# A mask built as bytes among the first constants, two PSUM banks held from one unit earlier, and new orders on all engines

## The chip, the cores and the metric

The kernel runs on one core of one Trainium2 chip. The metric is the device time of one execution in microseconds. The kernel is one straight program: nothing loops at run time on the path that is taken, and each engine (TensorE = PE, VectorE = DVE, ScalarE = ACT, GpSimd = POOL, and SyncE = SP, which issues all DMAs) works through its own list of instructions in a fixed order and waits on semaphores for the others.

## The reference, cut to what matters

```python
def _attn_ref(q, k, v, a_re, a_im):            # (B=4, H=8, S=768, D=48)
    mag = sqrt(a_re**2 + a_im**2); scale = minimum(mag, 0.999) / (mag + 1e-6)
    ar, ai = a_re * scale, a_im * scale
    for t in range(S):                          # complex state S_re, S_im of D x D for each head
        new_re = ar[t, :, None] * S_re - ai[t, :, None] * S_im
        new_im = ar[t, :, None] * S_im + ai[t, :, None] * S_re
        S_re, S_im = new_re + outer(k[t], v[t]), new_im
        y[t] = q[t] @ S_re
def _moe_ref(x, w_in, w_out):                   # x: 3072 x 384, w_in: 384 x 2048, w_out: 2048 x 384
    h = x @ w_in
    return (h * tanh(softplus(h))) @ w_out
```

The first part is a linear recurrence with a complex decay for each row of the state; its output, with the heads side by side, is the x of the second part. The weights come as 8-byte whole numbers that hold doubles, and are turned into floats on the chip.

## The kernel before

The 768 time steps of a batch are cut into 3 units of 256 steps, so there are 12 units, each of two chunks of 128 steps. A unit goes through three stages, and all engines work on several units at once:

- **The decay** (`ew_steps`): the magnitude and the angle of the decay are summed along time (DVE scans), and q and k are multiplied by growth and by cosine and sine. ACT needs two of its function tables for it: one with logarithm and exponential (`l`), one with sine and arctangent (`t`). Line 240 asks for each load of a table by name (`SETS`, `l` and `t` in turn, 43 loads). Within a unit the angle's arctangent needs `t`, the magnitude's Ln and Exp need `l`, the sines need `t` again. For unit 0 the two chunks (g = 0, 1) go apart. The products with sine and cosine (line 466, tiles X and QK) are laid out anew by SP's DMAs as tile T (line 462, three DMAs of X and three of QK for each chunk), which has 96 rows for each head.
- **The attention of a chunk** (`attn_steps`): PE turns k (`pkn`, line 553; ACT copies it to `kn`, line 554), multiplies k by q (`pa`, line 597; from unit 3 on in 32-row pieces, line 592), DVE masks the result into `am` (line 599 with the causal mask `cmask`; from unit 3 on by a predicated copy through `turned_mask`, line 593, into an `am` that was zeroed before), PE makes the output (`ypsum`, line 612; ACT copies it to `y`, line 617) and the state's update (`pd`, line 632; DVE makes S of it, lines 637 to 640). SP sends y on as `xf` (lines 653, 666).
- **The two dense layers** (`moe_steps`): 8 pairs of columns a unit; PE `ph` (lines 695, 699), a chain on ACT and DVE (lines 703 to 709, tiles e, g, gh, gl), PE `po` (lines 732, 736). In units 0 and 1 half of the work uses the weights `raw` as whole floats; the others use two parts (`w`) that DVE and ACT cut them into (`divide`). Before that, each of the 16 blocks of weights is made a float by ACT (line 278), DVE (lines 280, 281) and POOL (line 283).

PE also runs 84 matmuls on nothing (`junk`, line 516: 40 that wait for the first angle, 44 more), which keep it busy. What stands in a row on an engine is set by hand: the table `ORDER` holds one list of numbers for each engine, and `in_order` ties each instruction to the one before it in the list.

PSUM banks: `bank` (line 530) gives the attention its banks under the tag `pa`, of which there are two. Up to unit 2 each use takes a new tile of the pool; from unit 3 on (`PU` = 3) two tiles are held for good and used in turn, and DVE sets each to zero when it is taken (line 535). The mask for the predicated copy is made when unit 3 first needs it: POOL sets an `am` (floats) to one, cuts it with eight selects, casts it to bytes, and sets the two `am` to zero (lines 577 to 585).

Of the kernel before, what the change touches and what calls it, by code (L numbers as in the profile page):

```python
# [120 lines left out]
    """,  # L121
    "DVE": """
# [70 lines left out]
    """,  # L193
}

SETS = "l t l t l t l t l t l t l t l t l t l t l t l t l t l t l t l t l t l t l t l t l t l"

# [798 lines left out]
```

## Time and profile before

| | us |
|---|---|
| median of 3 runs | 573.54 (572.95 to 574.87) |
| the profiled execution | 572.68 |
| its span in the trace | 570.9 |

| engine | busy, us | share of the span |
|---|---|---|
| PE | 545.7 | 96% |
| DVE | 475.6 | 83% |
| ACT | 467.4 | 82% |
| POOL | 46.5 | 8% |

The trace counts times from the start of the span. A row of the timeline merges a run of like instructions and tells in brackets how long the engine stood idle ahead of it and what ended that. A row of a window tells how long each engine was busy in one stretch. Since PE works in a fixed list, its end is the start of its first true matmul, plus its work, plus the time that it then waits.

### The profile page before, as it was taken

The numbers are of one execution on the slowest core, as the hardware profiler recorded it, in microseconds if no ns is written. First come the engines' busy times: TensorE is split into PE (matmuls) and PEld (weight loads), VectorE is DVE, ScalarE is ACT, GpSimd is POOL, SyncE is SP. The second block draws the span as 40 slices with busy tenths as digits, with TensorE's granted clock in tenths as the row PEclk, the third lists the DMA queues.
The fourth block names the chain that finished last, engine by engine and source line by source line (L and its number), as shares of the span: only waits on it lengthen the run. The fifth ranks groups of instructions, "written<-read, shape, count | busy, mean of one in ns | idle before, by whom it ended". The sixth has DMA issues, their size and how long they took to land.

```text
span 570.9 us, 14394 instructions
## 1 busy us (share of the span) xinstructions
PE 545.7 (96%) x5830; PEld 506.1 (89%) x5830; DVE 475.6 (83%) x795; ACT 467.4 (82%) x749; POOL 46.5 (8%) x60
## 2 busy tenths in 40 slices
PE   0799999999999999999999999999999999999996
PEld 0367877889999999999999999999999999999996
DVE  5999999999999898887989899777897788545543
ACT  7899898999979899978898997787988867646571
POOL 2022322234002000000000000000000000000000
PEclk9999999999999999999999999999999999999999
DMA  8666865815655645606635727517334535301000
GB/s 296 225 195 220 311 195 151 239 56 148 188 172 153 189 155 142 187 28 170 190 108 141 200 74 214 149 38 220 93 109 125 160 99 147 112 30 29 3 26 32
DMA packets 69063, 81.65 MB, mean 143 GB/s; under 512 B 6144, under 2 KB 60672, under 8 KB 68992
## 3 DMA queue, kind: packets, MB, share of 16 engines
q1 hardware_dynamic: 68992, 80.68, 48.2%
q8 instruction: 47, 0.77, 0.6%
q14 instruction: 24, 0.20, 0.1%
HBM read 45.51 MB, written 11.40 MB: 100 GB/s over the span
## 4 chain that ended last, share of the span: by engine, by line
PE 64%; DVE 13%; ACT 12%; DMA 5%; issue 3%; SPq 2%; DVEq 0%; ACTq 0%
PE po L736 27%; PE ph L699 27%; PE ypsum L612 5%; PE pp L592 3%; ACT L240 3%; DMA raw<-w_out 2%; PE pp L632 2%; DVE g L709 2%; DVE X L419 1%; DVE w L249 1%; DMA raw<-w_in 1%; ACT R L482 1%; DVE gl L249 1%; SPq L462 1%; DMA T<-X 1%
## 5 line engine op out<-in xcount | busy, mean ns | idle before, releaser
L699 PE MATMUL ph<-xH,w 128*128 128x256 f32 x1104 | 216.4, 286 | 0.5 <-DVE g L709 0.4
L736 PE MATMUL po<-w,gh 128*128 128x384 f32 x704 | 193.6, 339 | 0.0
L699 PEld LDWEIGHTS ph<-xH,w 128*128 128x128 f32 x1104 | 177.6, 191 | 3.8 <-issue 1.2
L699 PE MATMUL ph<-xL,w 128*128 128x256 f32 x552 | 156.9, 284 | 0.3 <-DVE xL L249 0.3
L736 PEld LDWEIGHTS po<-w,gh 128*128 128x128 f32 x704 | 127.6, 188 | 1.3 <-issue 0.6
L736 PE MATMUL po<-w,gl 128*128 128x384 f32 x352 | 118.2, 337 | 0.0
L699 PEld LDWEIGHTS ph<-xL,w 128*128 128x128 f32 x552 | 105.2, 191 | 2.0 <-DVE xL L249 0.9
L703 ACT ACTIVATE e<-ph 128x512 f32<-128x512 f32 (+1 forms) x100 | 57.2, 573 | 37.2 <-PE ph L699 32.6
L705 ACT ACTIVATE e<-e 128x512 f32<-128x512 f32 (+1 forms) x100 | 60.8, 611 | 30.8 <-DVE e L704 30.7
L709 DVE SCALAR_TENSOR_TENSOR g<-e,ph 128x512 f32<-128x512 f32 (+1 forms) x100 | 65.7, 660 | 19.6 <-ACT e L707 18.3
L736 PEld LDWEIGHTS po<-w,gl 128*128 128x128 f32 x352 | 66.1, 188 | 0.3 <-DVE gl L249 0.2
L249 DVE TENSOR_TENSOR gl<-g,gh 128x512 fp32r<-128x512 f32 x88 | 59.9, 684 | 5.6 <-ACT gh L248 5.3
L707 ACT ACTIVATE e<-e 128x512 f32<-128x512 f32 (+1 forms) x100 | 60.9, 612 | 2.1
L706 ACT ACTIVATE e<-e 128x512 f32<-128x512 f32 (+1 forms) x100 | 60.9, 611 | 1.8
L704 DVE TENSOR_SCALAR e<-e 128x512 f32<-128x512 f32 (+1 forms) x100 | 41.1, 413 | 24.2 <-ACT e L703 23.7
L240 ACT ACT_TABLE_LOAD x43 | 55.2, 1283 | 1.6 <-PEq L950 0.8
L516 PE MATMUL junk<-cmask 128*128 128x512 bf16 x84 | 23.1, 419 | 14.3 <-DVE I L425 14.3
L283 POOL TENSOR_TENSOR raw<-raw 128x768 int32<-128x768 int32 x16 | 26.7, 1675 | 87.2 <-DVE raw L281 29.1
L612 PE MATMUL ypsum<-T,S 96*48 96x128 f32 x320 | 32.3, 277 | 0.0
L516 PEld LDWEIGHTS <-cmask 128*128 128x128 bf16 x84 | 8.7, 106 | 24.1 <-issue 17.9
L593 DVE COPY_PREDICATED am<-tmask,pp 128x512 f32<-128x512 uint8 x36 | 25.8, 734 | 4.3 <-PE pp L592 4.3
L248 DVE CAST gh<-g 128x512 fp32r<-128x512 f32 x48 | 20.6, 429 | 10.2 <-PE po L736 10.0
(103 smaller groups left out, 848.6 us busy)
## 6 DMA issues: line engine op xcount, KB each, us to landing
T<-X SPq DMA_DIRECT2D x72, 129.0 KB, 2.6
T<-QK SPq DMA_DIRECT2D x72, 129.0 KB, 2.5
raw<-w_in SPq DMA_DIRECT2D x8, 768.0 KB, 6.4
raw<-w_out SPq DMA_DIRECT2D x8, 768.0 KB, 7.4
kd<-vx SPq DMA_DIRECT2D x45, 128.0 KB, 2.2
kn<-kd SPq DMA_DIRECT2D x15, 384.0 KB, 3.3
V<-v SPq DMA_DIRECT2D x12, 384.0 KB, 5.2
out_dram<-o SPq DMA_DIRECT2D x24, 192.0 KB, 2.5
```

The source lines that it names most:

```text
L240: nc.scalar.preload_act_table_set({"l": "natural_log_exp_and_others", "t": "trig_and_small"}[name])
L249: leng(out=lo, in0=src, in1=h.bitcast(F32), op=ALU.subtract)
L516: ins = nc.tensor.matmul(junk, cmask, cmask.unsqueeze(1).broadcast_to([P, 4, P]), start=True, stop=True)
L612: nc.tensor.matmul(py[64 * par:64 * par + D, i, :], lhs, rhs, start=n == 0, stop=first or n == 1)
L699: nc.tensor.matmul(ph[:, a, :], rows_in(parts[j][:, wp], kt, a), st[xp][:, kt, :], start=n == 0, stop=n == 8)
L703: act(e, ph, AF.Exp)
L704: nc.vector.tensor_scalar_min(e, e, math.exp(20.0))
L705: act(e, e, AF.Square, bias=1.0)
L706: act(e, e, AF.Ln, scale=0.2, bias=0.2)
L707: act(e, e, AF.Exp, scale=-1.0)
L709: nc.vector.scalar_tensor_tensor(g, e, 2.5, ph, ALU.subtract, ALU.mult)
L736: nc.tensor.matmul(po[t], gp[:, a, tsl], rows_out(parts[NPAIR + j][:, wp], a), start=j in starts and a == 0 and n == 0, stop=j + 1 in ends ...
```

## The change

1. `turned_mask` is made among POOL's first constants, as bytes (int8, read as uint8 by the copy): one memset and eight selects on bytes. The memset to one, the eight selects on floats and the cast in unit 3 are gone; the two memsets of `am` to zero stay.
2. `bank` holds its two tiles from unit 2 on (`u >= PU - 1`), which writes them whole first; DVE's two memsets of line 535 are gone.
3. `SETS` has two more table loads, 45 for 43.
4. `ORDER` has new lists. PE's list is another up to entry 2102 (some 200 us into the span) and the same from there on; it holds the same instructions, 84 `junk` among them. The lists of DVE, ACT, POOL and SP are another over about the same stretch.

```diff
 ORDER = {
     "PE": """
-        0+20 48+4 40+4 52+4 20+2 56+4 44+4 60+15 22+13 124+4 75+5 128+2 35 132+4 130 188+6 36+2 226+3 38 80+5 136+4 85
+        0+20 40+2 48+6 44 54+2 20+3 56+8 45+3 42+2 23+12 64+12 124+6 35 76+4 132+4 36 188+6 130 226 131 248 80+10
...
-SETS = "l t l t l t l t l t l t l t l t l t l t l t l t l t l t l t l t l t l t l t l t l t l"
+SETS = "l t l t l t l t l t l t l t l t l t l t l t l t l t l t l t l t l t l t l t l t l t l t l"
...
-    turned_mask = const.tile([P, 4, C], U8, name="tmask")
+    turned_mask = const.tile([P, 4, C], mybir.dt.int8, name="tmask")
+    nc.gpsimd.memset(turned_mask, 1.0)
+    for i, lo, hi in ((0, 0, 128), (1, 0, 32), (1, 32, 64), (1, 64, 128), (2, 0, 64), (2, 64, 128), (3, 0, 96), (3, 96, 128)):
+        nc.gpsimd.affine_select(out=turned_mask[lo:hi, i], in_=turned_mask[lo:hi, i], compare_op=ALU.is_ge, fill=0.0,
+                                base=-((lo - 32 * i) % P), pattern=[[1, C]], channel_multiplier=-1)
...
         def bank(shape, use, name, c):
-            if u >= PU:
+            if u >= PU - 1:
                 if len(banks) < 2:
                     banks.append(ps.tile([P, 4 * C], F32, tag="pa", name="pp", bufs=2))
-                    nc.vector.memset(banks[-1], 0.0)
...
                             am = at.tile([P, 4, C], F32, tag="am", name="am", bufs=2)
-                            if not masked:
-                                nc.gpsimd.memset(am, 1.0)
-                                for i, lo, hi in (...):
-                                    nc.gpsimd.affine_select(out=am[lo:hi, i], ...)
-                                nc.gpsimd.tensor_copy(turned_mask, am)
                             nc.gpsimd.memset(am, 0.0)
...
-                        nc.vector.copy_predicated(am, turned_mask, pa)
+                        nc.vector.copy_predicated(am, turned_mask.bitcast(U8), pa)
```

What stands in a row at three places. The first is ACT in the opening, from the end of the first logarithms of unit 0 (X_145 or X_156 and X_146 or X_157 are unit 0's two work tiles, R and I its decay, raw the weights). Before:

```order
L370 ACTIVATE X_145<-X_145 128x384
L278 ACTIVATE raw_152<-raw_152 128x768
L406 ACTIVATE X_146<-R_139 128x3x128
L407 ACTIVATE X_146<-R_139 128x3x128
L240 ACT_TABLE_LOAD
L482 ACTIVATE I_140<-I_140 128x384
L368 ACTIVATE X,good<-R 128x3x128
L371 ACTIVATE X_146<-I_140 128x3x128
L368 ACTIVATE X,good<-R 128x3x128
L482 ACTIVATE R_139<-I_140 128x384
L482 ACTIVATE X_145<-I_140 128x384
L482 ACTIVATE R_139<-R_139 128x384
```

And of the change, from the same place (the lines are four later):

```order
L244 ACT_TABLE_LOAD
L486 ACTIVATE I_151<-I_151 128x384
L375 ACTIVATE X_157<-I_151 128x3x128
L282 ACTIVATE raw_163<-raw_163 128x768
L244 ACT_TABLE_LOAD
L410 ACTIVATE X_157<-R_150 128x3x128
L374 ACTIVATE X_156<-X_156 128x384
L411 ACTIVATE X_157<-R_150 128x3x128
L244 ACT_TABLE_LOAD
L486 ACTIVATE X_156<-I_151 128x384
L486 ACTIVATE I_151<-I_151 128x384
L486 ACTIVATE R_150<-I_151 128x384
```

The first arctangent (L482, now L486, of I) goes ahead of the magnitude's last exponentials, and that takes two more table loads; the second chunk's arctangent now stands with the first chunk's sines, behind the third of these loads. Behind the piece of the change come one more Square (L372), the last sine and a load.

The second place is SP in the opening, from the first DMA of T on. Before:

```order
L462 DMA T<-X_146 16x8x258
L324 DMA QK<-k 128x3x128
L324 DMA QK<-q 128x3x128
L462 DMA T<-X_146 16x8x258 x2
L462 DMA T<-QK 16x8x258 x3
```

And of the change, where the other load of q now stands among the first loads:

```order
L466 DMA T<-X_157 16x8x258 x3
L466 DMA T<-QK 16x8x258
L328 DMA QK<-k 128x3x128
L466 DMA T<-QK 16x8x258 x2
L321 DMA R<-a_re 128x768
```

One load, not two, now stands between the six DMAs that PE's first true work needs. The same place ahead of it has a load of q in third position, in front of the second load of R and the first weights.

The third place is POOL. Before, in unit 3:

```order
L578 MEMSET am 128x512
L283 TENSOR_TENSOR raw_1063<-raw_1063 128x768
L581 AFFINE_SELECT am<-am 64x128
L581 AFFINE_SELECT am<-am 32x128
L581 AFFINE_SELECT am<-am 96x128
L581 AFFINE_SELECT am<-am 32x128
L581 AFFINE_SELECT am<-am 128x128
L585 MEMSET am 128x512
L581 AFFINE_SELECT am<-am 32x128
L581 AFFINE_SELECT am<-am 64x128 x2
L584 CAST tmask<-am 128x512
L585 MEMSET am 128x512
```

And of the change, in the opening, from the last of the old constants (`ident`) to the first weights:

```order
masks.py:199 AFFINE_SELECT ident<-ident 96x96
L235 MEMSET tmask 128x512
L237 AFFINE_SELECT tmask<-tmask 128x128
L237 AFFINE_SELECT tmask<-tmask 64x128
L237 AFFINE_SELECT tmask<-tmask 32x128 x3
L237 AFFINE_SELECT tmask<-tmask 64x128
L287 TENSOR_TENSOR raw_163<-raw_163 128x768
```

The memset and six of the eight selects stand in the opening, ahead of POOL's first work on weights; the other two stand between later blocks of weights.

## Rows read from the trace of the kernel before

**Rows 1.** Windows: length; busy (count) of PE, PEld, DVE, ACT, POOL; clock, DMA, GB/s.
```profile
3.88:31.88 28.00, 13.60 (x76) 7.38 (x76) 25.12 (x54) 24.82 (x48) 1.46 (x1) 0.94 0.79 266
24.40:31.90 7.50, 6.73 (x56) 4.94 (x56) 7.44 (x17) 5.98 (x14) 0.00 (x0) 0.77 0.84 300
31.90:53.30 21.40, 20.39 (x187) 14.85 (x187) 21.26 (x41) 20.60 (x35) 5.30 (x4) 1.00 0.64 196
53.30:205.00 151.70, 150.67 (x1464) 133.78 (x1465) 148.35 (x242) 135.29 (x219) 32.87 (x30) 1.00 0.61 182
205.00:566.00 361.00, 361.00 (x4106) 350.12 (x4104) 279.69 (x458) 285.43 (x448) 5.01 (x14) 1.00 0.41 114
```

**Rows 2.** Timeline of PE: start, duration, line, operation, count, idle before, releaser.
```profile
24.43 1.13 PE L597 MATMUL pa<-T 96*128 96x128 f32 x8 [3.24 <-DMA T<-QK]
30.56 0.64 PE L612 MATMUL ypsum<-am,V 128*48 128x128 f32 x8 [0.70 <-DVE am L599]
37.66 0.54 PE L695 MATMUL ph<-xf,raw 128*128 128x128 f32 x3
53.31 0.60 PE L553 MATMUL pkn<-ident,T 96*128 96x96 f32 x5 [0.89 <-DMA T<-X]
117.30 0.36 PE L699 MATMUL ph<-xH,w 128*128 128x256 f32 x1 [0.36 <-DVE g L709]
189.56 0.39 PE L699 MATMUL ph<-xL,w 128*128 128x256 f32 x1 [0.33 <-DVE xL L249]
```

**Rows 3.** Timeline of ACT in the opening.
```profile
7.10 0.51 ACT L369 ACTIVATE X<-X 128x384 f32<-128x384 f32 x1
8.62 0.91 ACT L278 ACTIVATE raw<-raw 128x768 int32<-128x768 uint32 x1 [0.46 <-DMA raw<-w_in]
9.43 0.51 ACT L406 ACTIVATE X<-R 128x384 f32<-128x384 f32 x1
9.84 0.51 ACT L407 ACTIVATE X<-R 128x384 f32<-128x384 f32 x1
10.37 1.28 ACT L240 ACT_TABLE_LOAD   x1
11.66 0.52 ACT L482 ACTIVATE I<-I 128x384 f32<-128x384 f32 x1
31.88 0.59 ACT L617 COPY y<-ypsum 112x512 f32<-112x512 f32 x1
32.36 0.85 ACT L368 ACTIVATE X<-R 128x768 f32<-128x768 f32 x1
```

**Rows 4.** Timeline of DVE: the product QK of unit 0, and of unit 1.
```profile
17.23 0.96 DVE L466 TENSOR_TENSOR QK<-QK,R 128x768 f32<-128x768 f32 x1
47.16 0.95 DVE L466 TENSOR_TENSOR QK<-QK,R 128x768 f32<-128x768 f32 x1
```

**Rows 5.** Timeline of SP's queue: first and last DMA of unit 0's T.
```profile
16.86 0.71 SPq L462 DMA_DIRECT2D T<-X  x1
20.14 1.84 SPq L462 DMA_DIRECT2D T<-QK  x3
```

**Rows 6.** By line: DVE memsets and masked copies: ns min/median/max, first, last start.
```profile
L535 DVE MEMSET pp<- x2: 485/485/485, 128.3 to 138.6; 128x512 f32 x2
L593 DVE COPY_PREDICATED am<-tmask,pp x36: 708/734/754, 152.3 to 502.9; 128x512 f32<-128x512 uint8 x36
```

**Rows 7.** POOL: a constant's select, weights, unit 3's mask; DVE beside the weights.
```profile
1.76 0.29 POOL L230 TENSOR_SCALAR_AFFINE_SELECT cmask<-cmask 128x128 bf16<-128x128 bf16 x1
10.67 1.46 POOL L283 TENSOR_TENSOR raw<-raw 128x768 int32<-128x768 int32 x1 [8.13 <-DVE raw L281]
35.52 3.21 POOL L283 TENSOR_TENSOR raw<-raw 128x768 int32<-128x768 int32 x2 [23.39 <-ACT raw L278]
128.42 2.57 POOL L581 TENSOR_SCALAR_AFFINE_SELECT am<-am 64x128 f32<-64x128 f32 x5
35.59 1.82 DVE L280 TENSOR_SCALAR wx<-raw 128x768 uint32<-128x768 uint32 x1
```

More of the change, by code (lines that the diff above doesn't have):

```diff
@@ L75 @@
     "PE": """
[45 rows of a table removed]
[45 rows of a table added]
     """,
     "DVE": """
[27 rows of a table removed]
[27 rows of a table added]
     """,
     "Activation": """
[22 rows of a table removed]
[22 rows of a table added]
     """,
     "Pool": """
-        5 3+2 1 7 0 6 2 8 10 9 11 56 12+2 15 14 17 16 18+6 27 26 25 28 24 33 36 35 30 29 39 31 34 32 37+2 40+8 49 48
-        51 50 52+2 55 54
+        14 3+2 1 16 0 15 2 5+2 11 7 13 8+2 17 19 18 20+3 24 23 12 26+2 25 10 28+2 31 30 32 34 33 36 35 37+2 55 40 39
+        41+6 48 47 50 49 51+2 54 53
     """,
     "SP": """
[13 rows of a table removed]
[13 rows of a table added]
     """,
 }
-SETS = "l t l t l t l t l t l t l t l t l t l t l t l t l t l t l t l t l t l t l t l t l t l"
+SETS = "l t l t l t l t l t l t l t l t l t l t l t l t l t l t l t l t l t l t l t l t l t l t l"
 def in_order(tc, nc):
@@ L576, in f @@
                             am = at.tile([P, 4, C], F32, tag="am", name="am", bufs=2)
-                            if not masked:
-                                nc.gpsimd.memset(am, 1.0)
-                                for i, lo, hi in ((0, 0, 128), (1, 0, 32), (1, 32, 64), (1, 64, 128),
-                                                  (2, 0, 64), (2, 64, 128), (3, 0, 96), (3, 96, 128)):
-                                    nc.gpsimd.affine_select(
-                                        out=am[lo:hi, i], in_=am[lo:hi, i], compare_op=ALU.is_ge, fill=0.0,
-                                        base=-((lo - 32 * i) % P), pattern=[[1, C]], channel_multiplier=-1)
-                                nc.gpsimd.tensor_copy(turned_mask, am)
                             nc.gpsimd.memset(am, 0.0)
```

212 rows, old and new, of the table ORDER are left out of this document.

## The prediction, written before the change was run

> **What bounds the kernel now.** I read the windows first, for where PE waits, then PE's own timeline for what it waits for, then the opening on ACT, DVE and SP. PE's first true matmul starts at 24.43, behind 3.24 us of idleness that a DMA of T ends [rows 2]. From there on PE is idle for 7.50 - 6.73 = 0.77 us up to 31.9, 1.01 up to 53.3, 1.04 up to 205 and not at all after that [rows 1]: 2.8 us in all. The last 361 us are work alone. The change keeps PE's instructions, the 84 empty ones among them, so the end can move by three things only: the start at 24.43, these 2.8 us, and new waits of PE ahead of 205 us. DVE is the other full engine: 21.26 of 21.40 us busy, then 148.35 of 151.70 [rows 1], so what comes late from ACT or SP makes DVE late, and it has little room to catch up. ACT has some room: 24.82 busy of 28.00 us in the opening, so 3.2 us idle [rows 1].
>
> **The first rows of T.** Instructions of ACT on 384 columns start 0.41 us apart (9.43, 9.84), and a table load takes 1.28 us, with the next instruction 0.01 us behind it (10.37 to 11.66) [rows 3]. The new list switches at the end of the logarithm, 7.10 + 0.51 = 7.6. Load to 8.9; arctangent; Square; the copy of the weights' low part at 9.7 for 0.91 (its DMA had landed at 8.62, and now has one load of 192 KB more ahead of it: at the window's 266 GB/s 0.7 us, so 9.3, still in time); load from 10.6 to 11.9; three Exp, of which DVE holds none up, to 13.25; load to 14.5; sine, arctangent of the second chunk, Abs, Square, last sine, which ends near 16.9. DVE's product with it then ends near 17.9; before it ended at 17.23 + 0.96 = 18.19 [rows 4]. The other product (X) ends near 17.05. SP issued eight DMAs from 16.86 to 21.98, 0.64 us each [rows 5]; now the same stretch holds seven, from 17.07: 17.07 + 7 x 0.64 = 21.55. PE started 2.45 us behind the last issue, which gives 24.0. Term: **-0.43 us** on PE's first true work. Two loads more on ACT there cost 2.57 us, and what hides them is idle time and the second chunk's arctangent, which no longer needs a switch of its own.
>
> **From there to the first dense layer.** PE's first `ph` at 37.66 is a fixed point: it needs y, copied by ACT at 31.88, and DMAs behind that, 5.78 us in all [rows 2, 3]. Ahead of that copy ACT now does 2.57 us of loads and the Square that stood behind it (0.85 us and its accumulator), and leaves two copies of kn, 384 columns each, for later (0.41 us each): net 2.8 us. If all 3.2 us of idle time take it up, the copy starts at 31.5; if none does, at 34.7. Carried on by the same steps along ACT and DVE, I get 32.2, near the lower end, since the two longest waits of ACT in that stretch were for angles which now come earlier. So `ph` starts near 38.0: +0.3 us. The copies of kn come some 3 us later, so on PE the state's update waits; the new list has 12 empty matmuls ahead of it, and its result is needed only by the next chunk.
>
> **Unit 1, and DVE from there on.** The same steps put unit 1's first arctangent at 38.0 and its QK product at 46.7 to 47.65 where it was 47.16 to 48.11 [rows 4]; the last DMA of its T goes out 0.35 us earlier, and PE's wait at 53.31 [rows 2] ends at 52.95. There PE would be 0.35 us ahead. DVE is not: with its scan of the first magnitude behind the weights' DMA (about 1 us idle near 8.5) and two waits for exponentials, I find it 0.65 us behind at 53 us, for equal work. From 60 to 117 us its list holds the same work ahead of each product that PE takes (to within 0.3 us for `g`), so it stays behind by as much, and at 117.30, where PE already waited 0.36 us for `g` [rows 2], PE takes DVE's lateness over: **+0.65** at most, -0.35 at least. These are sums over some sixty instructions, good to about 1 us.
>
> **The memsets of the two banks** took 0.485 us each, at 128.3 and 138.6 [rows 6]: up to 0.97 us of DVE, less some overlap. That is more than the 0.65 us, and DVE is level from there. PE has no wait between 117 and 189, so it gains nothing directly; at 189.56 it waits 0.33 us for `xL` [rows 2], which hangs on a DMA of xf, and a PE that comes 0.65 later finds that wait gone. So of +0.65 about +0.3 is left.
>
> **The mask.** POOL's work at 128 us (five selects 2.57 us [rows 7], three more, a memset, a cast) goes; nothing waits for it, since the mask is first used at 152.3 [rows 6]. In the opening the memset and six selects are priced by the select of 0.29 us [rows 7]: about 2.3 us, done by 5, and POOL idles 8.13 us there, up to its first weights at 10.67 [rows 7]. What can cost there is DVE. One row shows a DVE instruction on 768 columns taking 1.82 us beside POOL's work on weights (35.59 beside 35.52 [rows 7]); one on as many columns with two inputs took 0.96 [rows 4], so at least 0.86 us was lost. With byte selects of 0.3 us such a meeting costs 0 to 0.3 us, and DVE waits for ACT in that stretch; I take 0.
>
> The Trainium skill has a rule for this (SBUF — State Buffer, section "Who interferes with whom"): a DVE instruction with two inputs in SBUF and a GpSimd instruction that reads SBUF shut each other out for a whole instruction. It speaks against moving the selects beside unit 0's first DVE instructions, which read R twice. By it the sum would get up to 0.3 us, as above.
>
> **The held banks.** Unit 2 uses two tiles in turn as it did two buffers, and a bank is still free when its last reader is done. If tracking inside one tile releases a region earlier or later, the bound is the 0.73 us of a masked copy [rows 6] either way; I take 0.
>
> **The sum.** From -0.35 to +0.65 at PE, with +0.3 after 189 us and nothing that moves the rest: between 572.3 and 573.3 against the profiled 572.68. Take +0.15; the profiled execution lies 0.86 below the median, so 573.7 for the median. That is no change: 0.3% is 1.7 us, about what a measurement can tell from none.
>
> **Rivals.** *Slower: the loads are not absorbed.* If ACT's idle time in the opening is not where the loads fall, y is copied up to 2.8 us late, `ph` starts late by as much, and PE has no slack afterwards to win it back: 573.5 + 2.8 = 576.3. It decides from a copy later than 33.6. For it: as I carry it on, ACT's new list has hardly a pause between 17 and 32. Against it: the second arctangent needs no wait now, and the wait of 0.46 us at 8.62 [rows 3] is filled. 0.22.
>
> *Slower by more: a switch costs more than its load.* If each switch cost as much again as its load, the two would take 5.1 us, 2 us over ACT's idle time at the very least, and y would come 2.2 to 5.4 us late: 575.7 to 578.9. Against it: the next instruction stands 0.01 us behind the load, with nothing idle ahead of it (9.84 + 0.51 = 10.35, load at 10.37) [rows 3]. 0.03. The Trainium skill (ScalarE: Activation LUTs, section "What ACT_TABLE_LOAD costs") is such a rule: 1283 ns for the load, and about 1380 ns for a drain with it. The row agrees with the load's time and shows no drain.
>
> *Faster: the new order takes PE's waits away.* All that PE can win is 0.43 + 2.8 = 3.2 us, 570.3; if the waits at 30.56, 53.31, 117.30 and 189.56 (0.70, 0.89, 0.36, 0.33 [rows 2]) go, that is 0.43 + 2.28 = 2.7, 570.8. For it: my sum has an error of about 1 us, the second mask (`am` of 30.56) comes earlier in it, and the clock, 0.77 in that window [rows 1], costs PE there something that closer work would give back. Against: more than half of all PE's waits must go, and `ph` hangs on y. 0.25.
>
> *The change does not do what it says.* The memsets and the selects are gone from the lists, so this is left only for the use of it: DVE's 0.97 us may be worth nothing since PE sets the end. My forecast has that in it.
>
> **How the numbers follow.** Forecast of no change 0.50, at 573.7, own range 572.0 to 575.2; faster by over 0.3% 0.25; slower by over 0.3% 0.25. The range 570.8 to 576.3 goes from the faster case's time to that of the slower one, and leaves out what is beyond either.
>
> **What would show it.** Right: T's first matmul near 24.0; four table loads before 14.5; y copied between 31.5 and 33; `ph` near 38; from 205 us on PE without a gap; `am` of unit 3 untouched by POOL at 128. Wrong: y copied after 33.6; a new wait of PE over 1 us between 24 and 140; PE's clock at its lower level (1.2 GHz) for longer than in the window from 24.4 to 31.9, since the new order leaves PE idle more between 26 and 29 us; DVE at 117 us later by more than 1.5 us, or earlier.

## The result, and the profile after

The changed kernel takes 576.03 us (median of 8 executions, 575.22 to 578.87); the kernel before takes 572.91 in the same comparison (8 executions, 571.89 to 574.87). The ratio is 1.0056, with a 95% interval of 1.0037 to 1.0076: **slower, by some 3.1 us**. That lies inside the range of the prediction, 0.3 us from its upper end, but it isn't the likeliest case. The profiled execution took 575.68 us with a span of 574.0 us, against 572.68 and 570.9.

The windows of the changed kernel, over the same stretches as [rows 1] (length; busy time and count of PE, PEld, DVE, ACT, POOL; clock, DMA, GB/s):

```profile
3.88:31.88 28.00, 12.82 (x62) 6.56 (x63) 24.35 (x54) 26.66 (x49) 3.02 (x6) 0.94 0.75 258
24.40:31.90 7.50, 5.79 (x42) 4.03 (x43) 7.50 (x20) 7.44 (x15) 0.00 (x0) 0.77 0.82 288
31.90:53.30 21.40, 19.95 (x194) 13.94 (x192) 21.20 (x40) 21.12 (x37) 5.33 (x3) 1.00 0.65 192
53.30:205.00 151.70, 149.50 (x1456) 131.73 (x1453) 146.78 (x238) 132.86 (x214) 26.61 (x23) 1.00 0.60 180
205.00:566.00 361.00, 360.32 (x4111) 350.20 (x4110) 280.82 (x461) 288.00 (x453) 4.21 (x14) 1.00 0.42 117
```

PE is idle for 1.71, 1.45, 2.20 and 0.68 us in the last four stretches; before it was 0.77, 1.01, 1.03 and 0 [rows 1]. That is 3.2 us more (0.94, 0.44, 1.17 and 0.68), which is the whole loss. The clock is the same as before in each stretch, so in this pair of executions it is no part of the difference. What PE waits for (engine, line, releaser: us, times, the longest):

```profile
PE junk L520 <- DVE I L429: 15.5, 1, 15.5
PE pkn L556 <- DMA T<-QK: 3.2, 1, 3.2
PE pkn L556 <- DMA T<-X: 2.0, 1, 2.0
PE ph L690 <- DMA xf<-y: 0.9, 1, 0.9
PE ypsum L607 <- DVE am L594: 0.7, 2, 0.4
PE ph L694 <- DVE g L704: 0.6, 2, 0.4
PE po L731 <- DVE gl L253: 0.2, 1, 0.2
```

Three rows of PE's timeline in the changed kernel:

```profile
25.75 0.35 PE L556 MATMUL pkn<-ident,T 96*128 96x96 f32 x2 [3.16 <-DMA T<-QK]
...
39.40 0.87 PE L690 MATMUL ph<-xf,raw 128*128 128x128 f32 x5 [0.91 <-DMA xf<-y]
...
55.77 0.27 PE L556 MATMUL pkn<-ident,T 96*128 96x96 f32 x1 [2.00 <-DMA T<-X]
```

The first true matmul comes at 25.75 and not at 24.43 [rows 2]: 1.32 us late; in the rest of that stretch PE then waits less than before. The wait for unit 1's T grew from 0.89 us [rows 2] to 2.00, and the first `ph` comes 1.7 us later, behind a DMA of xf. From 205 us on PE is idle for 0.68 us, mostly in waits for DVE, where before it never was.

The opening shows why it is late. DVE's timeline in the changed kernel:

```profile
6.49 0.56 DVE L370 SCALAR_TENSOR_TENSOR X<-R 128x384 f32<-128x384 f32 x1 [0.35 <-DMA R<-a_re]
9.68 0.56 DVE L284 TENSOR_SCALAR wx<-raw 128x768 uint32<-128x768 uint32 x1 [1.15 <-DMA raw<-w_in]
13.74 1.19 DVE L380 TENSOR_TENSOR I<-I,X 128x384 f32<-128x384 f32 x1 [0.67 <-ACT X L374]
18.51 0.96 DVE L470 TENSOR_TENSOR QK<-QK,R 128x768 f32<-128x768 f32 x1
```

ACT's, in the same stretch:

```profile
10.15 0.53 ACT L375 ACTIVATE X<-I 128x384 f32<-128x384 f32 x1 [0.58 <-DMA I<-a_im]
10.58 0.88 ACT L282 ACTIVATE raw<-raw 128x768 int32<-128x768 uint32 x1
```

And POOL's, the selects of the mask and the first weights, with one of the selects by itself (count, ns min/median/max, start):

```profile
3.08 2.61 POOL L237 TENSOR_SCALAR_AFFINE_SELECT tmask<-tmask 128x128 int8<-128x128 int8 x6
...
L237 POOL TENSOR_SCALAR_AFFINE_SELECT tmask<-tmask x1: 624/624/624, 3.4 to 3.4; 64x128 int8<-64x128 int8 x1
...
13.04 1.47 POOL L287 TENSOR_TENSOR raw<-raw 128x768 int32<-128x768 int32 x1 [7.35 <-DVE raw L285]
```

Three loads come late in this profile, behind the load of q in third place: the second chunk's R (0.35 us of waiting on DVE), the first weights (1.15 us on DVE) and the second chunk's I (0.58 us on ACT). The two waits on DVE are not what sets line 380: DVE stands idle for 0.67 us more ahead of it, for an exponential of ACT, and ACT is late by its wait for I. Then this product takes 1.19 us where a like one, not beside POOL, takes 0.55 (7.97 us, same line); POOL adds up the first weights at that moment, because they came late. DVE starts its product QK at 18.51, not at 17.23 [rows 4]: 1.28 us late, about the sum of 0.58 and 0.64.

How late the opening is differs from one execution to the next. unit1_rows below has the same opening lists; in its profile neither R nor I is waited for, the weights' first step on DVE starts at 9.03, QK at 17.86, and PE's first true matmul at 24.60.

### The profile page after: what moved, and what is told of

Same layout as the page of the kernel before. It is cut to its first block, busy times and chain, and to the rows that moved or that the text cites. A ratio compares the mean times of both kernels' runs of the same rounds, so it can differ in the third digit from the quotient of the medians.

```text
span 574.0 us, 14392 instructions
## 1 busy us (share of the span) xinstructions
PE 545.6 (95%) x5830; PEld 505.1 (88%) x5830; DVE 474.9 (83%) x793; ACT 469.9 (82%) x751; POOL 42.2 (7%) x59
## 4 chain that ended last, share of the span: by engine, by line
PE 70%; DVE 11%; DMA 6%; ACT 6%; SPq 4%; issue 2%; DVEq 0%; ACTq 0%
PE ph L694 29%; PE po L731 28%; PE ypsum L607 5%; PE pp L587 3%; SPq L466 3%; PE po L727 2%; PE pp L627 2%; DMA T<-X 2%; ACT L244 1%; DMA I<-a_im 1%; DMA xf<-y 1%; DVE g L704 1%; DVE R L406 1%; DVE e L699 1%; DVE QK L470 1%
## 5 line engine op out<-in xcount | busy, mean ns | idle before, releaser
L252 ACT CAST gh<-g 128x512 fp32r<-128x512 f32 x40 | 24.4, 610 | 7.6 <-PE po L731 5.3
```

## The experiments

Each kernel was timed beside the kernel before, in 6 to 12 executions. Times are medians in us; "before" is the kernel before in the same comparison. A profile shows one of these executions, so its span can be far from the median.

| kernel | time | before | ratio | 95% |
|---|---|---|---|---|
| the change | 576.03 | 572.91 | 1.0056 | 1.0037 to 1.0076 |
| parts_old_lists | 576.29 | 573.31 | 1.0044 | 1.0027 to 1.0060 |
| q_load_back | 576.08 | 573.31 | 1.0047 | 1.0029 to 1.0066 |
| raw_step_later | 578.65 | 573.31 | 1.0102 | 1.0077 to 1.0127 |
| q_back_raw_later | 579.10 | 573.31 | 1.0091 | 1.0064 to 1.0118 |
| mask_old_lists | 572.49 | 572.89 | 0.9996 | 0.9985 to 1.0007 |
| banks_other_turn | 572.70 | 572.89 | 0.9997 | 0.9988 to 1.0006 |
| turn_more_empty | 573.06 | 572.89 | 1.0002 | 0.9991 to 1.0012 |
| q_back_unit1_rows | 573.44 | 572.89 | 1.0021 | 1.0005 to 1.0036 |
| unit1_rows | 575.45 | 572.66 | 1.0042 | 1.0027 to 1.0056 |
| old_unit1_rows_new | 572.58 | 572.66 | 0.9997 | 0.9987 to 1.0006 |
| old_q_third | 575.11 | 572.66 | 1.0038 | 1.0026 to 1.0051 |
| three_moves | 573.79 | 572.67 | 1.0024 | 1.0009 to 1.0038 |

### The parts without the new lists

**parts_old_lists** has the byte mask and the held banks of the change, with the lists and the 43 loads of the kernel before (numbers adapted to the instructions that are gone).

```diff
 (the change)
-SETS = "l t ... l"   # 45 loads, ORDER of the change
+SETS = "l t ... l"   # 43 loads, ORDER of the kernel before
```

> Parts 1 and 2 of the change alone (byte mask among POOL's first constants, banks held from unit 2, no memsets), with the old 43 table loads and the old lists; only two of the byte selects stand between later weights, as in the change. Theory A (the loss of 3.1 us lies in the new lists): PE's first matmul of T at 24.4, the wait for X at 53.3 near 0.9, total 572 to 573.5, a ratio to the kernel before of 0.998 to 1.001. Theory B (the loss lies in the byte selects beside DVE's first instructions, or in what the held banks make PE wait for): PE's first matmul later than 25, or new waits of PE in unit 2, total near 576.

It is as slow as the change, without the change's lists. So theory A's time fell, and the second half of theory B holds. But that doesn't clear the new lists: the opening here is as before (first matmul at 24.56), and the loss stands in unit 2, where the change has none. Of what PE waits for, the second longest after the start is new:

```profile
PE pp L592 <- ACT kn L557: 2.3, 1, 2.3
```

PE's timeline has it here:

```profile
105.16 1.16 PE L592 MATMUL pp<-T 96*128 96x128 f32 x8 [2.29 <-ACT kn L557]
...
106.15 4.48 PE L727 MATMUL po<-raw,g 128*128 128x384 f32 x8
```

In the kernel before, the row that answers to the second of these, right behind the masked product, is:

```profile
103.18 2.87 PE L732 MATMUL po<-raw,g 128*128 128x384 f32 x8
```

ACT's copy that PE waits for, again in parts_old_lists:

```profile
104.65 0.45 ACT L557 COPY kn<-pp 128x384 f32<-128x384 f32 x1
```

And two of its windows (columns as above):

```profile
100.00:105.00 5.00, 2.81 (x22) 2.48 (x21) 5.00 (x8) 4.12 (x7) 1.51 (x2) 1.00 1.03 267
...
106.00:110.00 4.00, 4.00 (x10) 2.27 (x10) 4.00 (x6) 3.56 (x6) 1.84 (x2) 0.57 1.02 314
```

PE stands still for 2.29 us, until ACT has copied the turned k out of the bank that the masked product wants. One us later the granted clock is near its lower level (0.57 of full speed in that window; 1.2 of 2.4 GHz is 0.5), and eight matmuls that took 2.87 us in the kernel before take 4.48. In this profile the wait costs twice: 2.29 us and then 1.6. The executions show it too: of the 12, the three at 573.80 to 574.75 us have a mean clock of 0.996 or 0.997, and of the nine at 576.01 or more eight have 0.990 to 0.992.

**mask_old_lists** and **banks_other_turn** take the two parts asunder. The first has the byte mask alone. The second has both parts, but for one use of a bank:

```diff
-        def bank(shape, use, name, c):
+        def bank(shape, use, name, c, again=False):
             if u >= PU - 1:
-                if len(banks) < 2:
+                if again:
+                    pass
+                elif len(banks) < 2:
...
-                    pa = bank([P, 4, C], "am", "pa", c)
+                    pa = bank([P, 4, C], "am", "pa", c, u == PU - 1 and c == 0 and g == 1)
```

> Part 1 of the change alone (the byte mask among POOL's first constants), with the old lists, the old 43 table loads and the banks held from unit 3 with their two memsets. Theory D (the 2.3 us of PE's wait near 105 us, and the clock that falls behind it, come from the banks alone): no new wait of PE, total as before, 572.5 to 573.8, ratio 0.999 to 1.001. Theory B (the byte selects disturb the opening): first matmul of T later than 24.9, total 574.5 or more.

> Parts 1 and 2 with the old lists, and the held banks taken in another turn: the second masked product of unit 2's first chunk takes the bank of the first one again, not the one in which the turned k still waits for ACT. Theory D1 (the wait of 2.29 us near 105 us is for that one bank, since held banks are taken strictly in turn): the wait is gone, and with it the fall of the clock behind it, total 572.0 to 573.3, ratio 0.997 to 1.001; with the two memsets of DVE gone too it may be some tenths under the kernel before. Theory D2 (held banks make PE wait anyway, for whatever was in them last): a wait of 1 us or more stays near 100 to 110 us, total 574.5 to 576.5.

Both are level with the kernel before. The mask costs nothing and gives nothing: its selects in the opening end at 5.59 us, and DVE's product QK starts at 17.13 and not 17.23. With the other turn PE has no wait over 0.9 us after its first matmul; so the wait was for that one bank (theory D1). Held banks are taken strictly in turn, and the turn gave the second masked product the bank whose turned k had not been copied yet, while the other had been read at 100 us. The pool of the kernel before had not made PE wait there. The two memsets that go with the held banks are worth nothing that this measures under the old lists.

**turn_more_empty** adds 12 empty matmuls behind the first 20, to keep the clock up while PE waits for T.

```diff
-WREP, WREP2, WK = 40, 44, -9.4
+WREP, WREP2, WK = 52, 44, -9.4
 "PE":
-        0+20 48+4 40+4
+        0+32 60+4 52+4
```

> As the kernel with the other turn, and 12 more empty matmuls behind the first 20, which fill some 2.6 of the 3.2 to 4.1 us in which PE waits for the first rows of T. Theory E (idle time of PE brings its clock to the lower level, and that costs time in the end): the granted clock stays at 1.00 through 24 to 32 us, PE's first products take 1.1 us in place of 1.7 to 2.0, total 0.5 to 1.5 us under the kernel with the other turn alone, with less scatter. Theory E2 (what the clock costs there is hidden, since DVE sets the pace up to 53 us): clock at 1.00, total the same within 0.4 us.

The clock does stay up in that stretch, PE comes through it faster, and the time is the same (theory E2). Its windows:

```profile
24.40:31.90 7.50, 4.93 (x55) 3.90 (x56) 7.45 (x17) 5.98 (x13) 0.00 (x0) 1.00 0.85 304
31.90:53.30 21.40, 21.27 (x189) 15.00 (x186) 20.04 (x38) 20.00 (x35) 5.29 (x4) 0.92 0.60 186
```

PE's timeline, a little later:

```profile
30.80 0.64 PE L609 MATMUL ypsum<-am,V 128*48 128x128 f32 x8 [2.24 <-DVE am L596]
```

PE's products ended sooner, and it then waited 2.24 us for `am` (0.70 before [rows 2]), and the clock fell behind that wait instead. DVE sets the pace here: it is busy for 7.45 of 7.50 us with the same 17 instructions as before.

### The opening, in the change and in the old lists

**q_load_back** moves one entry of SP's list in the changed kernel, **raw_step_later** one of DVE's, **q_back_raw_later** both.

```diff
 "SP":
-        0+2 6 2 8 3 16 5 11 4 9 15 17
+        0+2 2 8 3 16 5 11 4 9 15 6 17
 "DVE":
-        41 7 14 42 15 19 16 9 13 10 20 8 28 17
+        41 7 14 15 19 16 9 13 10 20 8 42 28 17
```

> The changed kernel with one entry of SP's list moved: the load of the second chunk's q goes from third place behind the second load of V. Theory A1 (that load delays R, the weights and I behind it): the second chunk's I no longer holds ACT up at 10.15 (0.58 us there gone), the weights land 0.6 to 0.7 us earlier, PE's first matmul of T at 25.1 in place of 25.75, and if the lateness of the opening is carried to the end, 575.3 in all. Theory A2 (the opening's order on ACT and DVE costs it, not the loads): first matmul within 0.2 of 25.75, total 576. Theory C (what is lost in unit 1 is lost there, whatever the opening does): first matmul earlier, total 576 all the same.

> The changed kernel with one entry of DVE's list moved: the second step of the first weights (line 285) goes behind the product of line 449, so that POOL's part of the weights no longer runs beside DVE's product of line 380 (1.19 us at 13.74, where one alone takes 0.55). Theory A3 (the two share a way into SBUF, and this stretches the chain to X): line 380 takes 0.55 us, X's product starts 0.6 us earlier, PE's first matmul at 25.1 to 25.2; the same meeting may turn up later on another instruction. Theory A2' (the 1.19 us are hidden by the last sine, which QK waits for): first matmul stays within 0.2 of 25.75.

> Both moves together. Theory A: first matmul of T near 24.5, as in the kernel before, and total lower by what is carried, near 574.7; what is left against the kernel before (572.9) is then lost later, in unit 1's T (wait of 2.0 us near 53.4) and in the dense layers. Theory C: total 576 whatever the opening.

In the opening all three did what theory A says. With q back, I no longer holds ACT up and the first matmul comes at 25.02. With the weights' step moved, DVE's product of line 380 takes 0.56 us and not 1.19. With both, the first matmul comes at 24.37 and DVE's product QK starts at 17.23, exactly as before. And the time did not follow, and both theory A (near 574.7) and theory C (576) miss it: no gain that this measures from q alone, and longer times in the two others (for q_back_raw_later the interval overlaps that of the change). What PE waits for `am` in raw_step_later:

```profile
PE ypsum L607 <- DVE am L594: 3.4, 3, 1.7
```

DVE's timeline there:

```profile
14.02 0.56 DVE L380 TENSOR_TENSOR I<-I,X 128x384 f32<-128x384 f32 x1 [1.43 <-ACT X L374]
...
19.04 0.95 DVE L285 SCALAR_TENSOR_TENSOR raw<-raw,wx 128x768 uint32<-128x768 uint32 x1
```

The step's 0.95 us, which stood in DVE's idle time before 13 us, now stands in a stretch where DVE has none, and PE waits 3.4 us for `am` (0.7 in the change). In q_back_raw_later that wait is 2.1 us, and the clock comes on top:

```profile
31.90:53.30 21.40, 21.34 (x180) 14.69 (x182) 18.66 (x37) 18.80 (x34) 3.86 (x2) 0.85 0.60 178
```

Here PE is full at 0.85 of the clock and DVE is not. In both kernels the longest executions have the lowest mean clock: in raw_step_later 579.67 to 580.87 us go with 0.983 to 0.986, and 576.70 to 577.63 with 0.994. So an early start of PE was worth nothing by itself in these runs. Where the step stands on DVE cost PE its waits for `am`; how much of the longer times is these waits and how much the clock is not settled.

**old_q_third** asks the opposite: the kernel before, with only this load of q put in third place.

```diff
 "SP":
-        0+3 8 3 16 5 4 9 17 11 15 18 7 6 20 19
+        0+2 6 2 8 3 16 5 4 9 17 11 15 18 7 20 19
```

> The kernel before with only the load of the second chunk's q moved to third place on SP, as in the change. Theory A: the second chunk's I and the weights land 0.5 to 0.7 us later, but there is one DMA less between those of T, so PE's first matmul stays within 0.4 us of 24.43; as with the changed kernel, the end doesn't feel the opening: total 572.5 to 573.5, ratio 0.999 to 1.001. Theory A-end (a late opening is carried to the end): total 573.5 to 574.

This one entry makes the kernel before slower by 0.38%, some 2.2 us in the mean of 11 executions. The profile shows one of the shorter of them (573.73 us, with a span of 572.0, 1.1 more than before). DVE's timeline:

```profile
6.91 0.56 DVE L366 SCALAR_TENSOR_TENSOR X<-R 128x384 f32<-128x384 f32 x1 [0.88 <-DMA R<-a_re]
...
11.45 1.44 DVE L449 COPY X<-X 128x6 f32<-128x6 f32 x1 [0.20 <-ACT X L407]
...
18.38 0.95 DVE L466 TENSOR_TENSOR QK<-QK,R 128x768 f32<-128x768 f32 x1
```

ACT's:

```profile
9.66 0.92 ACT L278 ACTIVATE raw<-raw 128x768 int32<-128x768 uint32 x1 [1.07 <-DMA raw<-w_in]
```

And PE's:

```profile
24.74 1.13 PE L597 MATMUL pa<-T 96*128 96x128 f32 x8 [2.02 <-DMA T<-QK]
...
31.71 1.10 PE L612 MATMUL ypsum<-am,V 128*48 128x128 f32 x8 [2.42 <-DVE am L599]
```

R holds DVE up for 0.88 us, the weights arrive 1.04 us later than in [rows 3], and DVE starts its product QK 1.15 us late. PE's first matmul is late by 0.31 us only, as expected, since one DMA fewer goes out ahead of it. But DVE has no room to catch up: `am` comes late, PE waits 2.42 us for it, and the end is late by 1.1 us in this execution. Theory A had the opening right and the end wrong; theory A-end fits this execution, and the median lies above both. Of the six longest executions (575.11 us or more) five have a mean clock of 0.989 to 0.994, of the five shorter ones four have 0.994 to 0.997; no profile of a longer one was kept.

### Unit 1's T

**q_back_unit1_rows** and **unit1_rows** move one entry of SP's list of the change by two places, the first with the load of q moved back too; **old_unit1_rows_new** gives the kernel before the order of the change there.

```diff
 "SP", unit 1's first T:
-        31 35 33 30 34 32
+        31 30 35 33 34 32
```

> The changed kernel with the load of q moved back, as in the kernel of that name, and with the DMAs of unit 1's first T in the old order: two of X, three of QK, one of X (the change has X, two of QK, X, QK, X). Theory F (that order makes unit 1's T late): SP no longer idles between X and QK near 48 us, the wait of PE for X near 53 us falls from 1.56 to 0.5 to 1.1 us, total 574.8 to 575.5. Theory F2 (T waits for DVE's products, not for SP's order): wait still 1.4 to 1.6, total 576.

> The changed kernel with one entry of SP's list moved by two places: the second DMA of X of unit 1's first T goes ahead of the two of QK, as in the old list. The load of q stays in third place. Theory F (this entry makes unit 1's T late and PE wait 2.00 us there): PE's wait for X near 54 us falls to 1.0 to 1.4 us, total 573.4 to 574.6. Theory G (it takes both, the earlier opening and this entry): wait still 1.6 to 2.0, total 575.5 to 576.

> The kernel before with unit 1's first T sent off in the order of the change: X, two of QK, X, QK, X in place of two of X, three of QK, X; all else as before. Theory F: the last X goes out some 0.4 to 1.8 us later, PE waits 1.3 to 2.7 us for it in place of 0.89, and where the wait grows towards 2 us the clock falls in some executions; total 573.4 to 575.5. Theory F2 (the order of these six does nothing, the products are late): wait 0.9, total 572.9.

SP's queue in the change (start, duration, DMA, count):

```profile
47.68 0.62 SPq L466 DMA_DIRECT2D T<-X  x1
48.74 1.24 SPq L466 DMA_DIRECT2D T<-QK  x2
50.02 0.61 SPq L466 DMA_DIRECT2D T<-X  x1
50.67 2.13 SPq L466 DMA_DIRECT2D T<-QK  x1
52.85 1.91 SPq L466 DMA_DIRECT2D T<-X  x3
```

The same stretch of SP's queue in q_back_unit1_rows:

```profile
46.49 1.26 SPq L466 DMA_DIRECT2D T<-X  x2
47.92 2.66 SPq L466 DMA_DIRECT2D T<-QK  x3
50.62 1.92 SPq L466 DMA_DIRECT2D T<-X  x3
```

In the change SP stands idle from 48.30 to 48.74, with a second DMA of X ready to go but behind QK in its list. With both moves the last X of this T goes out at 50.62 and not at 52.85, and PE waits 0.86 us for it and not 2.00. The time falls from a ratio of 1.0056 to 1.0021, and the two intervals just don't touch. The entry alone gives 1.0042, q alone 1.0047; neither is told apart from the change. What PE waits for in unit1_rows, where the load of q stays in third place:

```profile
PE ypsum L607 <- DVE am L594: 3.0, 3, 1.3
...
PE pkn L556 <- DMA T<-X: 1.0, 1, 1.0
```

So the entry alone halves the wait for X, as theory F says, but PE now waits 3.0 us for `am` (0.7 in the change), and the time that theory F forecast, 573.4 to 574.6, does not come: the profiled execution has 574.31, the median is 575.45. In the old lists the order of these six moves the last X by 0.3 us and the wait to 1.2, and the time not at all. So the two together give back about 2 us of the 3.1, and how much belongs to each is not settled.

The opening of q_back_unit1_rows and of q_load_back is the same list. In the profile of the first, DVE's second step of the weights stood at 10.42, POOL had added them up by the time of line 380 (0.56 us), and DVE's product QK started at 17.14; in the second that step stood at 11.36, POOL met line 380 (1.14 us), and QK started at 18.00. So whether the two meet differs from one execution to the next, and single profiles of these kernels differ by some 0.9 us through it.

**three_moves** adds a third move that should keep them apart always: the weights' second step on DVE right behind the first.

```diff
 "DVE":
-        41 7 14 42 15 19
+        41 42 7 14 15 19
```

> The changed kernel with three entries moved: the load of q back behind the second load of V, the second DMA of X of unit 1's first T ahead of QK, and DVE's second step of the first weights (line 285) right behind its first step, so that POOL's part runs at about 11 to 12.5 us, beside DVE's scans, and not beside line 380. Theory H (DVE's lateness in the opening is carried on by DVE's full list up to 53 us, and sets the end): line 380 takes 0.55 us near 13.2, DVE's product QK of unit 0 starts near 17.4 (18.51 in the changed kernel, 17.23 before), total 572.4 to 573.2, ratio 0.999 to 1.001. Theory H2 (the new lists are slower for another reason, later on): QK near 17.4 and total still 573.4 or more, as with two moves.

Its timeline of DVE:

```profile
11.22 2.16 DVE L423 TENSOR_TENSOR_SCAN X<-rmask,I 128x384 f32<-128x384 uint8 x1
...
13.69 0.55 DVE L380 TENSOR_TENSOR I<-I,X 128x384 f32<-128x384 f32 x1
```

And of POOL:

```profile
10.87 1.70 POOL L287 TENSOR_TENSOR raw<-raw 128x768 int32<-128x768 int32 x1 [5.30 <-ACT raw L282]
```

The meeting only moved: now a scan takes 2.16 us (0.93 in the change), and QK starts at 17.83, not near 17.4. So this run doesn't test theory H: its condition was not met. It is as fast as with two moves. The Trainium skill (SBUF — State Buffer, section "Who interferes with whom") says that a DVE instruction with two inputs in SBUF and a GpSimd instruction that reads SBUF shut each other out; the product at 1.19 and the scan at 2.16 agree.

With two or three moves the new lists stay 0.2% behind the old ones. The profile of q_back_unit1_rows does not show why: it is the shortest of 11 executions, 572.89 us, level with the kernel before, and the two waits for DVE after 205 us that it keeps (0.71 us) are made good before that, where PE is idle for 0.52 us and not 1.03. These two windows are its:

```profile
53.30:205.00 151.70, 151.18 (x1468) 133.85 (x1469) 147.97 (x243) 133.51 (x216) 24.57 (x23) 1.00 0.59 177
205.00:566.00 361.00, 360.29 (x4107) 350.20 (x4106) 279.32 (x457) 286.28 (x450) 3.81 (x14) 1.00 0.42 117
```

Of the 11 executions of q_back_unit1_rows three took 575.61 to 576.86 us, with a mean clock of 0.989 to 0.991, and the others 572.89 to 573.82, with 0.993 to 0.997. The three make most of the 0.2%; what lowers the clock in them no profile shows. The two table loads were not run without the new lists, nor the new lists without the held banks.

No kernel that was run is faster than the kernel before by more than a measurement tells.

## Why the prediction was right and wrong, point by point

**The number.** 573.7 was forecast as no change, 0.15 us more than the kernel before; 576.03 was measured, 3.1 us more. That it lies inside the range is luck as far as the mechanism goes. The slower side had 0.25. The rival with that time (loads on ACT not absorbed, 576.3) is not what happened: it decided from a copy of y later than 33.6, and the copy came at 32.69.

**The first rows of T (-0.43 forecast, +1.32 measured).** This is the step that failed. Its sentence was that the weights' DMA "now has one load of 192 KB more ahead of it", 0.7 us, "still in time". The load of q was costed against the weights alone. It also stood ahead of the second chunk's R and I: 0.35 and 0.58 us of waiting [the opening above], and the wait for I is on ACT's way to line 380. DVE's idle time behind the weights was seen (about 1 us in the prediction, 1.15 measured), but it was carried on only as lateness at 53 us and not into the two products: that of QK was to end at 17.9 and started at 18.51. ACT's fourth load came at 14.14 and not at 13.25. And POOL's sum of the weights met a DVE product, for 0.64 us more: the price stood in [rows 7] (1.82 us), but it was weighed for the byte selects, which did no harm, and not for the sum of weights that the new order moved. With the same opening lists unit1_rows had its first matmul at 24.60, so the 1.32 us vary by execution; late it is in both, and not 0.43 early.

**Which engine's start counts.** The working led from PE's first matmul to the end. old_q_third shows, in one profile, a first matmul 0.31 us late and an end 1.1 us late; turn_more_empty shows a PE that comes through the stretch faster, and the same end. That DVE is full up to 53 us was in the prediction (21.26 of 21.40 us [rows 1]); the sum should have followed DVE's lateness from 6 us on. It did carry 0.65 us of it, but to a wait for `g` at 117 us. In the change PE has no wait there; it had paid by 55.77, in the wait for unit 1's T.

**From there to `ph`.** The copy of y was forecast at 32.2 and came at 32.69; with q back it comes at 32.2. So ACT's idle time did absorb the two loads. But `ph` came at 39.40, not 38.0: SP's new list has two DMAs of T and a load of I (0.59 us) ahead of xf, which goes out 1.54 us behind the start of y's copy and not 0.61. The fixed 5.78 us were carried over without reading the new list there.

**Unit 1.** The end of the wait for T was forecast at 52.95 and came at 55.77. DVE's QK was forecast at 46.7 and came at 47.75; where the opening is level with before (q_back_unit1_rows) it comes at 46.6, so this is the opening again. Some 1 us more goes with SP's order, X and QK by turns (in unit1_rows, with QK at 47.59, the wait ends at 54.62), which the prediction didn't cost at all: each queue that a step is moved past has to be gone through here too. With both moves the wait still ends at 53.45, 0.5 us behind the forecast; that is open.

**The memsets and the mask.** Right: nothing for PE under the old lists (banks_other_turn, mask_old_lists). Four of the six selects took 0.28 to 0.29 us, as priced from the select of 0.29 [rows 7]. The two that ran beside DVE products with two inputs took 0.62 and 0.50, and one of those products 0.61 in place of 0.56, so here the meeting cost POOL more than DVE. All were done at 5.69, not 5. That DVE without the two memsets is level again from 128 us on was not tested.

**The held banks.** Taken as 0, with 0.73 us as the bound either way. Under the old lists they cost 2.29 us of PE and the clock behind it; the bound was wrong, because it took two tiles in turn for the same thing as two buffers of a pool. In the change the new list of PE turns k and multiplies in another order there, and no such wait is left. So the new lists avoid this wait, and lose about as much elsewhere: in the opening, in unit 1 and in the waits after 205 us.

**From 205 us on.** "Without a gap" was nearly right: 0.68 us of waits for DVE, whose list is another beyond that point too.

## What to carry to other kernels

Where a second engine is full for the whole opening, cost a moved load at every engine that waits for any load behind it, and follow the full engine, not the one that ends the program. Two buffers held by hand and used in turn are not the same as a pool of two: ask for each use which instruction last read the one whose turn it is. A wait on TensorE can cost twice: behind one of 2.29 us the clock cost 1.6 us more, behind one of 2.00 us nothing. And one profile is one execution: set it against the times of the others before a wait in it is called the loss.

## What the runs showed that was not expected

- The same first 20 empty matmuls took 6.89 us in the profile of before, 7.05 in that of the change, 6.12 in parts_old_lists, 5.98 in q_load_back and 7.26 in old_q_third, from the same idle state. With it changes how long PE then waits for T (3.2 to 4.1 us in the first four of them) and how long the clock stays low after that: in 24.40 to 31.90 it is 0.77 in the profile of before and 0.54 in that of old_unit1_rows_new, which has the same lists up to there (6.19 us for the 20). The two executions took 572.68 and 572.76 us all the same. What sets it is open.
- The first weights' copy on ACT starts between 8.09 (mask_old_lists) and 8.85 us (turn_more_empty) under one and the same list of loads. With q in third place the weights' landing shows at 9.03 (unit1_rows), 9.66 (old_q_third), 9.68 (the change) and 9.92 (raw_step_later).
- POOL's add holds up more than DVE instructions with two inputs: in old_q_third a DVE copy of 6 columns took 1.44 us beside it, 0.17 in the kernel before.
- Behind a wait of 2.29 us the clock was at its lower level for some 3.4 of the 4 us from 106 to 110 (0.57 in that window, 0.5 being the lower level). The wait of 2.00 us in the profile of the change did not: the clock is 1.00 there.
